# Two sets of fifteen small loads on the load queue of a one-token attention and gated-MLP kernel

## The chip, the cores and the metric

The kernel runs on one core of one Trainium2 chip. The metric is device time in microseconds (us) of one execution, the median of repeated runs. The core has five engines, each with its own list of instructions: TensorE (PE, with PEld for its weight loads), VectorE (DVE), ScalarE (ACT), GpSimd (POOL) and SyncE (SP). They meet through semaphores alone. Loads from the chip's main memory (HBM) run on 16 DMA engines; here nearly all of them are issued by SP, and the page calls their queue q1.

## The reference

One token of width 576 goes through a layer norm, then through an attention over a cache of 8192 keys and values for each of 32 heads, and beside it through a gated MLP; both results are added to the token. Cut to what is computed:

```python
xn = layernorm(x)                                     # 1 x 576
q = (xn @ wq).reshape(32 heads, 128)
p = softmax(q . k_cache * 128**-0.5)                  # 32 heads x 8192 keys
o = p . v_cache                                       # 32 heads x 128
y = x + o.reshape(4096) @ wo + (relu(xn @ W_gate) * (xn @ W_up)) @ W_down
```

All of it is float32. The caches are 268 MB, the four weight matrices the rest of 319 MB, and each byte is used once.

## The kernel before

**Tiles.** The inputs are laid out so that almost every load is one tile of 128 partitions with up to 16384 floats in each (64 KB a partition, 8192 KB a load). Three SBUF tiles, slot0 to slot2, take the loads in turn. First come the query weights and two tiles with gate weights (wq, wqt, wg), then 32 loads from kv: load n brings the keys of head n and the values of the head before it. Then follows vw (values of the last head, the last gate weights and the first nine chunks of output weights, 7968 KB), and then the remaining 59 chunks of output weights from wod. OUT (line 25) cuts these into loads of 28, then 17, 8 and 3, then 2 and 1 chunks; one chunk is 128 x 576 floats, 288 KB.

**The load queue.** `load` (line 165) adds one DMA to SP's list, with a wait and a semaphore. SP works through its list strictly in order. A load waits until its slot is free, which is a mark on PE: ("pm", n - 3) for kv loads, ("pm", H - 2) for the load of 28 chunks, ("pm", H - 1) for those of 17, 8 and 3, and ("first", 8), set when the nine chunks that came with vw are used up, for those of 2 and 1. The last item of SP's list is the store of the result (line 190), which waits for the mark "end".

**A head.** DVE multiplies a tile of keys by the query (`product`, line 296) and sums over the head's width (`sums`, line 301), takes the maximum of each partition (line 302), PE spreads it and DVE reduces it (`bound`, line 305), ACT takes exponentials (`soft`, line 321), and PE multiplies by the values (`values`, line 328, all PE work at line 223). After three heads ACT copies the sums from PSUM to the tile `row` (`rows`, line 325) and PE turns them into columns (`outputs`, mark ("ot", k)). The last such group is k = NIT = 10, with the last two heads: its copy waits for the mark ("V", H - 1) of PE.

**The end.** PE multiplies every chunk of output weights by its column: the first 64 chunks into the bank `acc`, the last four into the bank `fin` (lines 409 to 431). DVE copies `acc` into the tile `both` (line 432, mark "y"), PE adds it to `fin`, DVE copies `fin` to `total4` (line 433, mark "end"), and SP stores it. The tile `both` has no other use, and `row` is not used after ("ot", NIT). A wait in the program is written as a mark; `run` (line 96) turns the marks of one instruction into semaphore waits, one for each semaphore.

Of the kernel before, what the change touches and what calls it, by code (L numbers as in the profile page):

```python
# [9 lines left out]
P = 128  # L10
# [8 lines left out]
NIT = (H - 2) // G  # L19
# [15 lines left out]
STEP = 1  # L35
# [6 lines left out]
class Program:  # L42
# [19 lines left out]
    def add(self, engine, f, waits=(), mark=None, on=None, by=1):  # L62
        to = None
        if mark is not None:
            to = on or engine
            self.sem(to)
            self.counts[to] += by
            assert mark not in self.marks, mark
            self.marks[mark] = (to, self.counts[to])
        self.lists[engine].append((f, tuple(waits), to, by))  # L70
# [41 lines left out]
def build(nc, x, kv, vw, wq, wqt, wg, wod, out):  # L112
    pr = Program(nc)
    add = pr.add

    def sb(name, shape):
        return nc.alloc_sbuf_tensor(name, list(shape), F32).ap()

    def bank(name):
        return nc.alloc_psum_tensor(name, [P, 512], F32).ap()  # L120
# [4 lines left out]
    both = sb("both", [P, N2])  # L125
# [12 lines left out]
    row = sb("row", [P, 576])  # L138
    xr = row[:1, :]
    row = row[:, :512]  # L140
    total4 = sb("total4", [P, Q])
# [12 lines left out]
    bq, bb, bm, bo, bt, acc, fin, bx = [bank(f"bank{i}") for i in range(8)]  # L154
# [3 lines left out]
    ot = bt[:, :G]  # L158
# [6 lines left out]
    def load(name, k, src, waits, on, start=0):  # L165
        dst = slots[k % 3][:, start:start + src.shape[-1]]
        add("sync", lambda e: e.dma_start(dst, src), waits, name, on=on, by=16)  # L167

    def tile(n):
        return slots[(n + 3) % 3]  # L170

    load("wq", 0, wq, (), "dwq")
    load("g0", 1, wqt, (), "dg0")
    load("g1", 2, wg, (), "dg1")
# [4 lines left out]
    for n in range(4, H):  # L179
        load(("t", n), n + 3, kv[n], (("pm", n - 3),), f"land{(n - 1) % G}" if n < H - 1 else "dlast")  # L180
    load(("t", H), H + 3, vw, (("pm", H - 3),), "dvw")
    f = OUT[0][0]
    for k, loads in enumerate(OUT[1:]):
        free = (("pm", H - 2), ("pm", H - 1), ("first", OUT[0][0] - 1))[k]
        i = 0
        for n in loads:
            load(("o", f), H + 4 + k, wod[:, (f - 9) * D:(f - 9 + n) * D], (free,), f"do{f}", i * D)
            i += n
            f += n
    add("sync", lambda e: e.dma_start(out.rearrange("o (j q) -> (o j) q", j=4), total4[0:P:32, :]), ("end",), "out", on="dout", by=16)  # L190


    add("gpsimd", lambda e: e.memset(ident, 0.0), (), "id0")
# [37 lines left out]
    for k in range(36):  # L231
        if k < 32:
            r, a, j = k // 16, k // 4 % 4, k % 4
            mm(("wq", "xz") if k == 0 else (), None, bq[32 * j:32 * j + 32, :], xz[:, a, 5 - r:37 - r],
               slots[0][:, a * 4096 + (4 * r + j) * 512:][:, :512], k < 4, False)
        else:
            j = k - 32
# [3 lines left out]
    def turn(rows, waits, mark):  # L241
        for b in range(4):
            add("tensor", lambda e, b=b: e.transpose(turned[:, b, :], rows[:, b * P:(b + 1) * P], ident),
                waits if b == 0 else (), mark if b == 3 else None)
# [77 lines left out]
                                             bias=nb[h % 2], scale=1.0, accum_out=L[:, i:i + 1]), waits, ("exp", h), on=f"exp{i}", by=STEP)  # L322

    def rows(k, h):
        add("scalar", lambda e: e.copy(row, bo), (("V", h),) + ((("ot", k - 1),) if k else ("pqt",)), ("oc", k), on="oc", by=STEP)  # L325


    def values(i, t, waits, mark, end):
# [22 lines left out]
    for n in range(1, H):  # L351
        k, i = (n - 1) // G, (n - 1) % G
        product(n, keys(n), i, (("t", n),) + ((("q", k + 1),) if i == 0 else ()))
        bound(n - 1)
        if i == 0 and k:
            close(k - 1, G)
        sums(n, keys(n))
        if i == 0 and k < NIT:
            spread(k + 2, [h for h in range(G * k + 4, G * k + 7) if h < H])
        soft(n - 1)  # L360
        if i == G - 1:
            rows(k, n - 1)
    bound(H - 1)
    soft(H - 1)
    rows(NIT, H - 1)
    add("vector", lambda e: e.tensor_copy(gr, bq), ("u3",), "gr")
    pj = turned.rearrange("k b (j r) -> k b r j", j=4)
# [15 lines left out]
    for i in range(G):  # L383
        t = tile(i + 1)
# [20 lines left out]
    f, end = 0, H + FC  # L405
# [3 lines left out]
    for k, loads in enumerate(OUT):  # L409
        t = tile(H)[:, SK + UNITS[3] * 512:] if k == 0 else slots[(H + 3 + k) % 3]  # L410
        i = 0
        for n in loads:
            for m in range(n):
                waits = (("o", f),) if m == 0 and k else ()
# [79 lines left out]
```

## Time and profile before

| what | value |
|---|---|
| median of 3 runs | 745.06 us (744.97 to 745.23) |
| profiled execution, span from first to last instruction | 743.7 us |
| median of the runs less that span | 1.3 us |
| DMA read | 319.16 MB, 429 GB/s over the span |
| busy time of DVE / PE / ACT / POOL | 575.6 / 294.7 / 36.2 / 1.8 us |
| mean granted TensorE clock | 0.674 |

The profile gives the span of its execution and no separate time for it; the runs' median is 1.3 us longer than the span. In the profile a releaser is what ended a wait. SPq and ACTq are the engines' own DMA issues; "us to landing" is counted from an issue until its semaphore is full. A window is a stretch of the span, in us from its start.

### The profile page before, as it was taken

How to read it: one execution, taken by the hardware profiler on the slowest of the kernel's cores; microseconds unless marked ns; L12 is line 12 of the kernel's file. 1: busy time of each engine (PE TensorE's matmuls, PEld its weight loads, DVE VectorE, ACT ScalarE, POOL GpSimd, SP SyncE). 2: the span in 40 equal slices, each digit the busy share in tenths (PEclk: the TensorE clock that was granted, in tenths of full speed). 3: DMA queues.
4: the chain of work that ended last, by engine and by line, in shares of the span. 5: the costliest groups of instructions: out<-in, count | busy, mean ns of one | idle time of the engine just before them, and what ended most of it. 6: DMA issues, size and time to landing. Idle time of an engine off the chain costs nothing.

```text
span 743.7 us, 4003 instructions
## 1 busy us (share of the span) xinstructions
PE 294.7 (40%) x1780; PEld 84.0 (11%) x1780; DVE 575.6 (77%) x169; ACT 36.2 (5%) x113; POOL 1.8 (0%) x9
## 2 busy tenths in 40 slices
PE   1555413253343343343343334324324324334677
PEld 1111100010010010010010001001001001001122
DVE  2000189989999999999999999999999999999610
ACT  2000000010010010010000000001001000000000
POOL 0000000000000000000000000000000000000000
PEclk9977756655565565665666666666566566566689
DMA  9999999999999999999999999999999999999997
GB/s 395 451 420 426 445 444 410 441 451 405 444 448 406 448 441 412 448 437 430 430 441 437 419 441 444 412 441 444 412 444 441 416 448 437 430 430 435 435 424 309
DMA packets 6066, 319.28 MB, mean 429 GB/s; under 512 B 677, under 2 KB 681, under 8 KB 1066
## 3 DMA queue, kind: packets, MB, share of 16 engines
q1 hardware_dynamic: 6056, 319.17, 99.3%
q8 instruction: 6, 0.10, 0.1%
q14 instruction: 2, 0.02, 0.0%
q10 hardware_dynamic: 2, 0.00, 0.0%
HBM read 319.16 MB, written 0.00 MB: 429 GB/s over the span
## 4 chain that ended last, share of the span: by engine, by line
DMA 58%; DVE 37%; PE 4%; issue 0%; ACT 0%; SPq 0%; DVEq 0%
DMA slot<-in_kv 47%; DVE slot L296 19%; DVE s L301 17%; DMA slot<-in_wqt 5%; DMA slot<-in_wod 5%; PE bank L223 4%; DVE mr L302 0%; DVE nb L305 0%; DVE total L310 0%; SPq L167 0%; ACT row L325 0%; DVE both L432 0%; ACT pzs L321 0%; DVE total L314 0%; DVE total L433 0%
## 5 line engine op out<-in xcount | busy, mean ns | idle before, releaser
L296 DVE TENSOR_TENSOR slot<-slot,bank 128x8192 f32<-128x8192 f32 x32 | 278.0, 8686 | 85.8 <-PE bank L223 50.5
L301 DVE TENSOR_REDUCE s<-slot 128x64 f32<-128x8192 f32 x32 | 277.6, 8676 | 0.0
L223 PE MATMUL bank<-slot,pzs 128*12 128x512 f32 x1024 | 181.2, 873 | 205.5 <-ACT pzs L321 205.5
L223 PEld LDWEIGHTS bank<-slot,pzs 128*12 128x12 f32 x1024 | 32.7, 122 | 332.2 <-ACT pzs L321 204.3
L223 PE MATMUL bank<-slot,xz 128*32 128x512 f32 x208 | 37.3, 753 | 31.7 <-DMA slot<-in_wq 12.8
L223 PE MATMUL bank<-ident,mr 128*128 128x128 f32 x64 | 16.3, 339 | 78.2 <-DVE mr L302 78.1
L223 PE MATMUL bank<-l,ones 128*128 128x3 f32 (+1 forms) x22 | 6.2, 354 | 99.9 <-ACT pzs L321 99.9
L321 ACT ACTIVATE pzs<-s,nb 128x64 f32<-128x64 f32 x32 | 11.1, 348 | 470.9 <-DVE nb L305 470.9
L246 DVE TENSOR_SCALAR row<-bank 128x512 f32<-128x512 f32 x1 | 0.7, 692 | 34.4 <-PE bank L223 34.4
L432 DVE COPY both<-bank 128x288 f32<-128x288 f32 x1 | 0.5, 459 | 27.2 <-PE bank L223 27.2
L223 PEld LDWEIGHTS bank<-ident,mr 128*128 128x128 f32 x64 | 9.9, 194 | 100.3 <-DVE mr L302 100.2
L283 ACT ACTIVATE dq<-ident,qs 128x128 f32<-128x128 f32 x32 | 10.7, 392 | 131.6 <-PE bank L223 90.9
L223 PEld LDWEIGHTS bank<-l,ones 128*128 128x128 f32 x22 | 5.3, 299 | 102.8 <-ACT pzs L321 102.0
L223 PEld LDWEIGHTS bank<-slot,xz 128*32 128x32 f32 x208 | 8.5, 133 | 57.7 <-issue 23.7
L223 PE MATMUL bank<-sel,row 128*128 128x3 f32 (+1 forms) x88 | 11.6, 254 | 7.3 <-ACT row L325 7.2
L223 PE MATMUL bank<-slot,os 128*1 128x288 f32 x128 | 10.8, 480 | 5.6 <-DMA slot<-in_wod 5.6
L223 PEld LDWEIGHTS bank<-sel,row 128*128 128x128 f32 x88 | 10.6, 191 | 16.8 <-ACT row L325 16.8
L223 PE MATMUL bank<-slot,hh 128*1 128x288 f32 (+1 forms) x160 | 12.0, 382 | 1.3 <-DMA slot<-in_wod 1.3
L223 PE MATMUL bank<-dq,ones 128*128 128x384 f32 (+1 forms) x24 | 11.4, 560 | 0.0
L223 PE MATMUL bank<-slot,xt 128*32 128x512 f32 x26 | 6.0, 896 | 9.8 <-DMA slot<-in_wqt 9.8
L325 ACT COPY row<-bank 128x512 f32<-128x512 f32 x11 | 6.5, 587 | 70.7 <-PE bank L223 70.7
L305 DVE TENSOR_REDUCE nb<-bank 128x1 f32<-128x128 f32 x32 | 9.1, 284 | 0.9 <-PE bank L223 0.9
(55 smaller groups left out, 52.4 us busy)
## 6 DMA issues: line engine op xcount, KB each, us to landing
slot<-in_wod SPq DMA_DIRECT2D x1, 8064.0 KB, 38.9
slot<-in_vw SPq DMA_DIRECT2D x1, 7968.0 KB, 39.2
slot<-in_wod SPq DMA_DIRECT2D x1, 4896.0 KB, 30.2
slot<-in_wod SPq DMA_DIRECT2D x1, 2304.0 KB, 35.7
slot<-in_wod SPq DMA_DIRECT2D x1, 864.0 KB, 37.2
slot<-in_wod SPq DMA_DIRECT2D x1, 576.0 KB, 25.7
slot<-in_kv SPq DMA_DIRECT2D x32, 39.7
slot<-in_wod SPq DMA_DIRECT2D x1, 288.0 KB, 26.0
```

Of the source, the lines that this page charges most:

```text
L223: add("tensor", lambda e: e.matmul(o, lhsT, rhs, start=start, stop=stop), waits, mark)
L246: add("vector", lambda e: e.tensor_scalar_mul(row, bq, SCALE), ("pq", "n7"), "qr")
L283: add("scalar", lambda e, m=m, h=h: e.activation(dq[:, m, :], ident, AF.Copy, scale=qs[:, h:h + 1]), (free,) if m == 0 else (), ("dq", k) ...
L296: add("vector", lambda e: e.tensor_mul(k3, k3, qb[:, m, None, :].to_broadcast([P, C, DH])), waits, ("mul", h))
L301: add("vector", lambda e: e.reduce_sum(s, k3, axis=AX.X), (("mul", h),), ("sum", h))
L305: add("vector", lambda e: e.tensor_reduce(nb[h % 2], pm, axis=AX.X, op=ALU.max, negate=True), (("pm", h),), ("nb", h))
L321: add("scalar", lambda e: e.activation(pz[:, i, :, 4 * G - 4:4 * G], s2[h % 2].rearrange("p (c b) -> p c b", b=4), AF.Exp, bias=nb[h % 2], ...
L325: add("scalar", lambda e: e.copy(row, bo), (("V", h),) + ((("ot", k - 1),) if k else ("pqt",)), ("oc", k), on="oc", by=STEP)
L432: add("vector", lambda e: e.tensor_copy(both, acc[:, :N2]), ("sums",), "y")
```

## The change

A helper `few` adds fifteen DMAs to SP's list, which load 15 rows, then 14, and so on down to 1 row, each into its own columns of a tile, and each with a semaphore of its own. It is called twice. Set a goes behind the load of vw: each row has 16 floats (64 bytes), the destination is `both`, there is no wait, and the last copy of `rows` (k = NIT) gets the fifteen marks of the set as waits. Set b goes behind the load of the last chunk: each row has 32 floats (128 bytes), the destination is `row`, each of its DMAs waits for ("ot", NIT), and the store of the result gets the fifteen marks of the set as waits. The source is always the start of wod; what the small loads bring is not read.

```diff
+    def few(name, t, n, waits=()):
+        for k in range(15, 0, -1):
+            add("sync", lambda e, k=k: e.dma_start(t[:k, (k - 1) * n:k * n], wod[:k, :n]), waits, ("few", name, k), on=f"few{name}{k}", by=16)
+
...
     load(("t", H), H + 3, vw, (("pm", H - 3),), "dvw")
+    few("a", both, 16)
     f = OUT[0][0]
...
-    add("sync", lambda e: e.dma_start(out.rearrange("o (j q) -> (o j) q", j=4), total4[0:P:32, :]), ("end",), "out", on="dout", by=16)
+    few("b", row, 32, (("ot", NIT),))
+    add("sync", lambda e: e.dma_start(out.rearrange("o (j q) -> (o j) q", j=4), total4[0:P:32, :]),
+        tuple(("few", "b", k) for k in range(15, 0, -1)) + ("end",), "out", on="dout", by=16)
...
     def rows(k, h):
-        add("scalar", lambda e: e.copy(row, bo), (("V", h),) + ((("ot", k - 1),) if k else ("pqt",)), ("oc", k), on="oc", by=STEP)
+        add("scalar", lambda e: e.copy(row, bo), (("V", h),) + ((("ot", k - 1),) if k else ("pqt",)) + (tuple(("few", "a", m) for m in range(1, 16)) if k == NIT else ()), ("oc", k), on="oc", by=STEP)
```

On SP, from the load of vw to the end, the list before was this (the last column pair is rows x floats in a row, and the square bracket names the semaphores waited for):

```order
L167 DMA slot<-in_vw 128x15936 [waits s_tensor]
L167 DMA slot<-in_wod 128x16128 [waits s_tensor]
L167 DMA slot<-in_wod 128x9792 [waits s_tensor]
L167 DMA slot<-in_wod 128x4608 [waits s_tensor]
L167 DMA slot<-in_wod 128x1728 [waits s_tensor]
L167 DMA slot<-in_wod 128x1152 [waits s_tensor]
L167 DMA slot<-in_wod 128x576 [waits s_tensor]
L190 DMA out_y<-total 4x144 [waits s_vector]
```

With the change the small loads of set b stand between the last load and the store; this is the end of SP's list now, from the load with 5 rows on:

```order
L174 DMA row<-in_wod 5x32 [waits s_tensor]
L174 DMA row<-in_wod 4x32 [waits s_tensor]
L174 DMA row<-in_wod 3x32 [waits s_tensor]
L174 DMA row<-in_wod 2x32 [waits s_tensor]
L174 DMA row<-in_wod 1x32 [waits s_tensor]
L196 DMA out_y<-total 4x144 [waits s_fewb7,s_fewb6,s_fewb8,s_fewb5,s_fewb9,s_fewb4,s_fewb10,s_fewb3,s_fewb11,s_fewb2,s_fewb12,s_fewb1,s_fewb13,s_vector,s_fewb14,s_fewb15]
```

The store's waits stand in the order in which SP meets them: the mark "end" (s_vector) comes fourteenth, and two of set b come after it. On ACT nothing is added but waits; these are its last five rows now, of which the last is the copy of `rows` for the last two heads:

```order
L290 ACTIVATE dq<-ident,qs 128x128 [waits s_tensor]
L328 ACTIVATE pzs,l<-s,nb 128x16x4 [waits s_tensor,s_vector] x3
L332 COPY row<-bank 128x512 [waits s_tensor]
L328 ACTIVATE pzs,l<-s,nb 128x16x4 [waits s_tensor,s_vector] x2
L332 COPY row<-bank 128x512 [waits s_fewa8,s_fewa9,s_fewa7,s_fewa10,s_fewa6,s_fewa11,s_fewa5,s_fewa12,s_fewa4,s_fewa13,s_fewa3,s_fewa14,s_fewa2,s_fewa15,s_fewa1,s_tensor]
```

The fifteen waits on set a come ahead of the wait for PE, which before was the copy's only one. PE, DVE and POOL have the instructions that they had, in the same order.

## The prediction

> **What bounds the kernel now.** First the page's head, its DMA row and its queues; then the chain of work that ended last.
>
> ```profile
> span 743.7 us, 4003 instructions
> DMA  9999999999999999999999999999999999999997
> DMA packets 6066, 319.28 MB, mean 429 GB/s; under 512 B 677, under 2 KB 681, under 8 KB 1066
> q1 hardware_dynamic: 6056, 319.17, 99.3%
> ...
> q10 hardware_dynamic: 2, 0.00, 0.0%
> 293.76 39.65 DMA slot<-in_kv
> ...
> 351.82 39.65 DMA slot<-in_kv
> ...
> 701.42 35.70 DMA slot<-in_wod
> 737.12 0.04 issue
> 737.16 2.66 PE bank L223 x40
> 739.83 0.02 issue
> 739.85 0.47 DVE both L432
> 740.32 0.04 issue
> 740.37 1.32 PE bank L223 x32
> 741.69 0.02 issue
> 741.71 0.31 DVE total L433
> ```
>
> SP's queue, q1, keeps the 16 DMA engines busy for 99.3% of the span, and no slice but the last is below 9 tenths. In the middle a wait ends at 293.76 + 39.65 = 333.41 and the next such one at 391.47, three loads later: 58.06 / 3 = 19.35 us for 8192 KB. So time on this queue is time of the kernel, up to the last load. The end is read from the timeline:
>
> ```profile
> 661.37 0.33 SPq L167 DMA_DIRECT2D slot<-in_vw  x1
> 680.71 34.88 SPq L167 DMA_DIRECT2D slot<-in_wod  x6
> 701.64 0.19 ACT L321 ACTIVATION_READ_ACCUMULATOR pzs<-s,nb 128x1 f32 x1
> 710.53 0.59 ACT L325 COPY row<-bank 128x512 f32<-128x512 f32 x1 [8.71 <-PE bank L223]
> 711.17 1.05 PE L223 MATMUL bank<-sel,row 128*128 128x2 f32 x8
> 719.65 6.83 PE L223 MATMUL bank<-slot,os 128*1 128x288 f32 x74 [4.90 <-DMA slot<-in_wod]
> 741.21 0.10 PEld L223 LDWEIGHTS bank<-slot,hh 128*1 128x1 f32 x8 [0.25 <-DMA slot<-in_wod]
> 741.71 0.31 DVE L433 COPY total<-bank 128x144 f32<-128x144 f32 x1 [1.40 <-PE bank L223]
> 742.04 0.62 SPq L190 DMA_DIRECT2D out_y<-total  x1
> ```
>
> The load of 28 chunks lands at 719.65, the last chunk at 741.21; PE waits for both. After the last chunk come 0.5 us of matmuls, DVE's copy until 742.02, and the store. The store's landing ends the span. A DMA delayed by some time before 741.21 delays the end by the same time; work behind the last chunk has 742.02 - 741.21 = 0.81 us of cover.
>
> **The change, part by part.** Nothing is removed. Each set adds 15 issues on SP and 15 + 14 + ... + 1 = 120 rows on q1, and how many marks these bring is shown by the two small DMAs of before: the one-row load of x is all of q10, with 2 packets, so one row and one mark. The store's packets are seen in two narrow windows:
>
> ```profile
> DMA packets 7, 0.00 MB, mean 29 GB/s; under 512 B 3, under 2 KB 7, under 8 KB 7
> q1 hardware_dynamic: 7, 0.00, 12.3%
> ...
> q1 hardware_dynamic: 1, 0.00, 2.8%
> ```
>
> The first (743.26 to 743.34) has four rows of 576 bytes and three marks: 12.3% of 16 x 0.08 us is 157 ns. The second (743.35 to 743.37) has the fourth mark alone: 2.8% of 16 x 0.02 us is 9 ns. So a row here costs (157 - 3 x 9) / 4 = 33 ns, a mark 9 ns, and a DMA has as many marks as rows when these are under 16. The small rows of 64 and 128 bytes are not in this trace: I bound one between the mark (9 ns) and the 576-byte row (33 ns), and take 12 ns, near the mark, since 64 and 128 bytes are nearer to 4 than to 576.
>
> *SP's issues.* A DMA right behind another took 0.43 us, the four-row store 0.62:
>
> ```profile
> 701.42 0.43 SPq L167 DMA_DIRECT2D slot<-in_wod  x1
> 714.79 0.81 SPq L167 DMA_DIRECT2D slot<-in_wod  x2
> ```
>
> Fifteen with 0.05 us between them take 15 x 0.48 = 7.2 to 15 x 0.67 = 10.1 us. Set a is issued from 661.7 to at most 671.8; what is queued behind it on SP is the load of 28 chunks, released at 680.71, so 8.9 us are left. Even if that load went out late, the queue has work until vw has landed, at 661.37 + 39.2 = 700.6 (the page's row for vw, below). Set b is issued behind the last load: 714.79 + 0.81 = 715.6, so until at most 725.7; its mark ("ot", NIT) is set at 711.17 + 1.05 = 712.22, earlier. Behind it stands only the store, released at 742.02. Price of both: nothing; without this cover an issue of over 1.7 us each (26.4 us / 15) would show.
>
> ```profile
> slot<-in_vw SPq DMA_DIRECT2D x1, 7968.0 KB, 39.2
> SPq L190 <- DVE total L433: 26.4, 1, 26.4
> ```
>
> *Set a on the DMA engines.* Its packets lie between vw and the next load on a queue that never idles, so they are paid in full on the engine that carries them. The worst placed engine gets one row of each of the 15 loads, an even spread gives 120 / 16 = 7.5. The price is 7.5 x (9 + 9) = 0.14 us at least where the slowest engine has an average share, 15 x (33 + 9) = 0.63 us at most, and zero if the engine that lands last is one that gets no rows. With 12 ns and all fifteen rows it is 15 x 21 = 0.31 us; I take **0.3 us**, and keep 0 and 0.63. The Trainium skill (DMA: Bandwidth & Descriptors, "Why a DMA increments its semaphore by 16 and not by 1") says that a queue like SP's takes the lowest-numbered engines, as many as the largest number up to 16 that divides the rows; the trace agrees on the number (four marks for four rows), and no row of it shows which engines. By that rule one engine has all fifteen rows and the sum is 0.31; by an even spread it would be 0.16.
>
> *The copy on ACT.* The waits on set a come first. Set a lands a fraction of a microsecond after vw, near 701; ACT is idle from 701.83 to 710.53 waiting for PE. The waits are over in that gap: nothing. Were they late by up to 8.7 us, nothing would move; behind the copy PE has another 4.9 us of idle before 719.65.
>
> *Set b.* It queues behind the last chunk. On the engine with all fifteen rows its last mark follows 0.31 us after that chunk, 0.63 at most, so it lands near 741.5 and at the latest at 741.84. The store's own mark "end" comes at 742.02: hidden, with 0.2 to 0.5 us to spare. Behind that mark two waits on set b remain, both satisfied: between 0 and 0.05 us, the step between two DMAs on SP; I take 0.
>
> Sum: 743.7 + 0.3 = 744.0 for the span, and with the 1.3 us around it, which the runs show, 745.06 + 0.3 = **745.4 us**. By the bounds 745.1 to 745.7, and the runs before spread over 0.26 us.
>
> **The rivals.** *First: each extra load costs a step of its own on the queue, beyond its packets.* The five loads from 719.65 to 741.21 move 31 chunks, 9.14 MB, in 21.56 us. At the pace of the kv loads (19.35 us for 8.39 MB, with one step in each) they would take 21.09; with four steps more than the kv loads' share the excess of 0.47 us makes at most 0.12 us a step. Fifteen steps are then 1.8 us for set a, and set b ends 1.8 us after 741.21, or 1.0 past the mark "end": 2.8 in all, **747.9**, slower. It crosses 0.2% (1.5 us, about what a measurement of this kernel can tell from no change) at 0.077 us a step. For it speaks the excess; against it that engines land unevenly, which gives an excess without any step. Chance 0.10.
>
> *Second: the marks are served one at a time.* If an engine held what is behind a mark until the rows ahead are confirmed, each small load would cost the time from the store's last packet, 743.36, to its landing at the span's end, 743.7: about 0.35 us. Fifteen make 5.2 us for set a, and 5.2 - 0.8 = 4.4 for set b: **754.7**. The Trainium skill (Perfetto Trace Analysis, "DMA Instruction — HWDGE (DVE, Sync)") says that the last descriptor of a DMA writes the semaphore only after the write before it is confirmed, and that this can be a surprisingly long delay. By that rule, if it holds up the queue, the time is this rival's; the trace speaks against the holding up, since a step costs 0.12 us at most there. Chance 0.05.
>
> *Third: the queue takes few loads at a time.* Six loads are out together in the trace (the six on wod, 701 to 716, with no long issue). Set a makes it 17 with the two big ones. If eight were the limit, SP would stall on set a until vw lands at 700.6, then issue its last eight in some 4 us and only then the load of 28 chunks, whose packets start about 1 us later: 5 us of idle queue. Set b would stall likewise and have seven issues left after 741.2: 3.5 us and a landing of about 1.2 more, 3.9 past "end". Sum 9, **754**. Chance 0.05.
>
> *Fourth: less than the packets.* The last engine carries none of the rows: 745.1. That lies within the forecast.
>
> **How the numbers follow.** Forecast, with the fourth case, 0.79: 744.9 to 746.5. First rival 0.10, second and third 0.10 together. Faster for a reason not seen, such as engines that end in another order, 0.01. The forecast alone leaves out 0.21, so the range takes in the first rival: 744.9 to 748.0. The first and the other rivals lie over the bound; a little of the forecast goes over either edge: faster 0.02, within 0.2% 0.80, slower 0.18.
>
> **What would show it.** The page has 6066 + 480 = 6546 packets, 677 + 480 = 1157 of them under 512 B. The load of 28 chunks is still issued at 680.7 and lands 0 to 0.6 us later than 719.65; ACT's last copy still waits for PE; the store's releaser is still DVE at line 433. A landing of vw's successor over 1.5 us late speaks for the first or second rival, an issue of a small load that lasts microseconds for the third, and a store released by a DMA says that set b outlived its cover. What would make the prediction wrong is any cost of a small load over 0.08 us on one engine.

## The result and the profile after

The changed kernel takes **748.34 us** (748.25 to 748.44, 4 runs) against 745.07 (744.97 to 745.23, 4 runs): 3.3 us slower, ratio 1.0043 with a 95% interval of 1.0032 to 1.0055. The forecast was 745.4, the range ended at 748.0. The profiled execution of the change took 748.25, with a span of 746.7, so 1.5 us lie outside the span where 1.3 lay before; the span itself grew by 3.0. The intervals below leave out one execution of set a alone, which took 1333.5 us.

The page's head, its DMA packets and its queues:

```profile
span 746.7 us, 4049 instructions
DMA packets 6547, 319.31 MB, mean 428 GB/s; under 512 B 1157, under 2 KB 1161, under 8 KB 1546
q1 hardware_dynamic: 6536, 319.19, 99.1%
...
q14 instruction: 3, 0.02, 0.0%
```

The 480 packets that were forecast are there, all under 512 bytes; one packet more is an instruction fetch on q14, which had two before. The timeline of the end, with the lines that answer to those of before:

```profile
661.59 0.33 SPq L167 DMA_DIRECT2D slot<-in_vw  x1
661.96 5.39 SPq L174 DMA_DIRECT2D both<-in_wod  x15
...
680.99 33.19 SPq L167 DMA_DIRECT2D slot<-in_wod  x6
...
709.11 0.59 ACT L332 COPY row<-bank 128x512 f32<-128x512 f32 x1 [7.54 <-PE bank L230]
...
714.22 11.91 SPq L174 DMA_DIRECT2D row<-in_wod  x15
...
720.77 7.31 PE L230 MATMUL bank<-slot,os 128*1 128x288 f32 x74 [7.45 <-DMA slot<-in_wod]
...
742.09 0.10 PEld L230 LDWEIGHTS bank<-slot,hh 128*1 128x1 f32 x8 [0.27 <-DMA slot<-in_wod]
742.59 0.31 DVE L440 COPY total<-bank 128x144 f32<-128x144 f32 x1 [1.41 <-PE bank L230]
745.00 0.62 SPq L196 DMA_DIRECT2D out_y<-total  x1
```

The load of 28 chunks is issued 0.28 us later than before (680.99 for 680.71), while vw still had 20 us to run, and PE has it 1.12 us later (720.77 for 719.65). The last chunk is 0.88 us late (742.09 for 741.21), and so is DVE's copy (742.90 for 742.02). Then SP, which went 0.02 us after that copy before, goes 2.10 us after it. From the store's issue to the end it is 1.7 us in both. So of the 3.0 us in the span 0.88 are set a's and 2.08 are the store's wait for set b. What SP waited for, and what the DMA engines did meanwhile, by the waits of SP and by windows (the last two numbers of a window are the DMA engines' busy share and GB/s):

```profile
SPq L106 <- DMA row<-in_wod: 17.9, 2, 17.7
...
739.00:741.70 2.70, 2.36 (x52) 0.93 (x44) 0.46 (x1) 0.00 (x0) 0.00 (x0) 1.00 0.56 205
741.70:745.00 3.30, 0.82 (x24) 0.21 (x13) 0.31 (x1) 0.00 (x0) 0.00 (x0) 1.00 0.00 0
```

All packets of set b have been started by 741.70, none is left, and yet SP is released only near 745: in these 3.3 us no data is left to move, and what SP still waits for are marks. The trace's records of semaphores show them. The last increments of the small loads' semaphores, from the load with 15 rows to that with one, and the length of the first packet of the load of 28 chunks on each of the 16 engines, in us:

```text
set a, last increment   700.82 700.99 701.16 701.33 701.51 701.68 701.84 702.04
                        702.25 702.44 702.13 702.30 701.96 702.14 702.18
set b, last increment   742.26 742.47 742.67 742.87 743.07 743.27 743.47 743.66
                        743.87 744.07 743.91 744.10 744.12 744.29 744.47
first packet behind set a, after    4.23 4.08 3.86 3.77 3.68 3.64 3.48 3.36
                                    2.81 2.65 2.48 2.41 2.40 2.40 2.39 2.39
first packet of that load, before   2.38 to 2.39 on all sixteen
```

Where two marks in a row are of one engine, they come in steps of 0.16 to 0.21 us, not of 9 ns (the list shows the last mark of each load, and jumps where that is another engine's). The first big packet behind set a is held by up to 1.85 us, in grades: from 4.23 to 2.48 in ten steps of 0.175 on the average. The starts of the packets ahead show which engine is which: fifteen small rows run ahead of the packet of 4.23, ten ahead of that of 3.64, five ahead of that of 2.48. The load's last landing, 720.73, is that of the engine with ten rows: the engine with fifteen was held longer, but had been about 1.2 us ahead of the last.

### The profile page after: what moved, and what is told of

The parts are those of the page before. It is cut to its first block, busy times and chain, and to the rows that moved or that the text cites. A ratio compares the mean times of both kernels' runs of the same rounds, so it can differ in the third digit from the quotient of the medians.

```text
span 746.7 us, 4049 instructions
## 1 busy us (share of the span) xinstructions
PE 298.9 (40%) x1780; PEld 84.1 (11%) x1780; DVE 575.5 (77%) x169; ACT 36.2 (5%) x113; POOL 1.8 (0%) x9
## 4 chain that ended last, share of the span: by engine, by line
DMA 57%; DVE 38%; PE 3%; issue 0%; SPq 0%; DVEq 0%
DMA slot<-in_kv 47%; DVE slot L303 19%; DVE s L308 18%; DMA slot<-in_wqt 5%; DMA slot<-in_wod 5%; PE bank L230 3%; DVE mr L309 0%; DVE nb L312 0%; SPq L167 0%; DVE total L317 0%; DVE both L439 0%; DVE total L321 0%; DVE total L440 0%; DVE os L322 0%; DVEq L106 0%
## 5 line engine op out<-in xcount | busy, mean ns | idle before, releaser
L230 PE MATMUL bank<-slot,pzs 128*12 128x512 f32 x1024 | 187.5, 900 | 204.1 <-ACT pzs L328 204.1
L230 PE MATMUL bank<-sel,row 128*128 128x3 f32 (+1 forms) x88 | 11.6, 254 | 7.3 <-ACT row L332 7.2
```

The lines of the kernel that those rows point to most:

```text
L230: add("tensor", lambda e: e.matmul(o, lhsT, rhs, start=start, stop=stop), waits, mark)
```

## The experiments

Theory M: on one engine the marks of small loads are served one after another, about 0.18 us each; some are absorbed, what lies behind more of them is held. What counts is the number of marks on the busiest engine, and how early that engine is through with the big loads. Rivals: R, the small rows are slow and the mark costs nothing; T, all marks go through one place, so their total counts; and, by sums, that each load costs the same wherever it stands. All runs are compared with the kernel before on the same chip (745.0 in each group); intervals are of the ratio. Edits are shown against the change, cut to the lines that matter.

**Each set alone.** `a_only` drops set b, `b_only` drops set a, each with its waits.

> Set a alone, no set b. All theories hold that the marks or rows of set a delay the load stream. Theory M (on each engine the mark of a small load holds what is behind it for about 0.18 us until its row is confirmed; reading ahead hides some of it): the load of 28 chunks lands about 1.1 us later than before and the end moves by 0.7 to 1.1 us, to 745.8 to 746.2. If set a costs only its packets (15 x 13 ns): +0.2, 745.3.

> Set b alone, no set a. Theory M: 15 marks of 0.18 us on the engine with all fifteen rows, so the last mark 2.5 to 2.8 us behind the last chunk at 741.2, near 743.9; then SP walks through its waits in up to 0.5 us: store at 744.0 to 744.5 instead of 742.04, so +2.0 to +2.5, 747.1 to 747.6. If sets a and b are independent, the gain of this run and that of set a alone add up to 3.3.

Set a alone: 746.12, ratio 1.0015 (1.0005 to 1.0025), as expected. Set b alone: 746.42, 1.0018 (1.0009 to 1.0028), which is 0.7 below what was expected. Together 2.5 by the medians, not 3.3: the sets do not look independent, though the intervals would allow it; the run on stacking below tests this. The trace of `b_only` says why its part was too high: the engine with all fifteen rows is one of those that end the last chunk early. Its last mark came at 742.30; the last mark of the set came at 742.99, on an engine that is late but has ten.

**Marks or rows.** `b_one_mark` loads 15 separate rows on each of 16 partitions with one DMA, so 240 rows, 15 of them and one mark on each engine; `a_one_mark` does the same in set a's place, with rows of 64 bytes.

```diff
-    few("b", row, 32, (("ot", NIT),))
+    add("sync", lambda e: e.dma_start(row[:16, :510].rearrange("p (c w) -> p c w", w=34)[:, :, :32],
+                                      wod[:16, :960].rearrange("p (c w) -> p c w", w=64)[:, :, :32]), (("ot", NIT),), ("few", "b"), on="fewb", by=16)
```

> Set b as one load: 16 partitions with 15 separate rows of 128 bytes each, so each engine has 15 rows but one mark. Theory M: one mark, so it lands about 0.4 us behind the last chunk, before the mark end: no change, 745.0 to 745.2. Theory R (a row under 512 bytes takes about 0.18 us to write, the mark nothing): 15 rows on every engine, the same 2.7 us behind the last chunk, store at about 744.0, 747.0.

> Set a alone as one load: 16 partitions with 15 separate rows of 64 bytes each, so every engine has 15 rows and one mark. Theory M (the marks): no packet behind it is held by over 0.2 us, 745.0 to 745.3 (15 rows of 13 ns add 0.2). Theory R (the rows): every engine is held as the busiest one of set a was, by 1.85 us, and the end moves by as much or more than with set a alone: 746.1 to 747.

745.37, 1.0004 (0.9994 to 1.0013), and 745.35, 1.0004 (0.9995 to 1.0013): twice the rows without the marks cost about 0.35 us, not told apart from nothing. R falls, for both sets: its 747.0 and 746.1 lie outside the intervals. The first packet behind `a_one_mark` is held by 0.15 to 0.33 us on the sixteen engines.

**The busiest engine or the total.** `b_one_row` makes every load of set b one row, so 15 rows and 15 marks in all.

```diff
-            add("sync", lambda e, k=k: e.dma_start(t[:k, (k - 1) * n:k * n], wod[:k, :n]), waits, ("few", name, k), on=f"few{name}{k}", by=16)
+            add("sync", lambda e, k=k: e.dma_start(t[:1, (k - 1) * n:k * n], wod[:1, :n]), waits, ("few", name, k), on=f"few{name}{k}", by=16)
```

> Set b as 15 loads of one row each: 15 rows and 15 marks in all, all on one engine. Theory M: what counts is the marks on the busiest engine, still 15; the last mark 2.5 to 2.8 us behind that engine's share of the last chunk, so +1.2 to +2.5 by where this engine stands among the sixteen: 746.3 to 747.6. Theory T (marks of all engines go through one place, 120 in 2.6 us, 22 ns each): 15 marks take 0.3 us and are hidden, 745.1.

745.66, 1.0009 (0.9999 to 1.0018): less than the band of M, more than T's. The time alone does not decide; the trace does. Its timeline, and the fifteen last increments of its loads:

```profile
740.88 0.11 PEld L229 LDWEIGHTS bank<-slot,hh 128*1 128x1 f32 x8 [0.24 <-DMA slot<-in_wod]
741.38 0.31 DVE L439 COPY total<-bank 128x144 f32<-128x144 f32 x1 [1.38 <-PE bank L229]
742.66 0.61 SPq L195 DMA_DIRECT2D out_y<-total  x1
```

```text
740.01 740.19 740.37 740.55 740.74 740.91 741.08 741.27 741.45 741.63 741.81 741.99 742.17 742.34 742.52
```

With nothing on the other engines the step is still 0.18 us, where T has 22 ns. The store goes 0.14 us after the last of them, 0.97 after DVE's copy. The engine that has the rows was through with the last chunk near 739.8, a microsecond before the latest (740.84), which hid that much of its 2.7 us. My band had allowed for too little of this lead.

**Stacking.** `a_one_row_b` has set b as in the change, and set a with one row in each load: `few` takes `m = k if name == "b" else 1` rows.

> Both sets, but set a as 15 loads of one row each, so that it puts its 15 marks on one engine and nothing on the others; set b as in the change. Theory M with stacking (both sets fall on the same engine, which set a makes late by 1.9 us and set b by 2.6 us more): last chunk lands about 0.6 us late, last mark of set b near 744.3, store at 744.3 to 744.9, so +2.5 to +2.9: 747.5 to 747.9. Additive theory (each set costs what it costs alone, set b 1.4 us, and set a with an eighth of its rows at most 0.6): 747.0 or less.

748.06, 1.0039 (1.0025 to 1.0053): nearly the whole loss comes back with an eighth of set a's rows. All five runs (747.78 to 748.40) lie above the additive theory's 747.0, which the interval just reaches; the trace decides. Behind set a one single first packet is held, with 4.22 us; the other fifteen take 2.38 to 2.39. At the end the latest landing of the last chunk is 742.08, and the fifteen marks of set b on one engine run from 742.27, one step behind it, to 744.78. So both sets fall on the same engine: set a uses up the lead that it had, and set b's fifteen marks follow on that. This agrees with the Trainium skill (DMA: Bandwidth & Descriptors, "Why a DMA increments its semaphore by 16 and not by 1"), by which a queue like SP's takes the lowest-numbered engines. The trace names no engine and shows only that it is the same one.

**How many are free.** `a_five` has five loads in set a (5 to 1 rows) and no set b; `b_eight` has eight in set b and no set a.

```diff
-        for k in range(15, 0, -1):
+        for k in range(5, 0, -1):
```

> Set a alone with five loads of 5 to 1 rows, so at most five marks on an engine. In the trace of the change the first packet behind set a was held by 1.85 us on the engine with the most marks and by about 0.18 less with each mark less, down to nothing at about four or five marks. Theory M with this allowance: no packet held by over 0.2 us, no change: 744.9 to 745.2. If each mark costs its share of the 1.1 us of set a alone: 745.35.

> Set b alone with eight loads of 8 to 1 rows. In the trace of set b alone the engines with few rows end the last chunk late, near 741.0, the one with all rows early, near 739.8. With eight loads the busiest engine is through at 739.8 + 8 x 0.18 = 741.3, the late ones with two marks or fewer at 741.5, all before the mark end: 745.0 to 745.3. If the cost goes with the number of loads: 8/15 of 1.4, 745.8.

745.10, 1.0000 (0.9991 to 1.0010), and 745.16, 1.0002 (0.9993 to 1.0011). Both as M has it. The medians lie below a cost in proportion (745.35 and 745.8), but the intervals reach that far; the traces speak against it. Behind five marks the first packet was held by 0.14 us at most, and the last chunk was not late (landed 741.10, before 741.17). In `b_eight` the last mark came at 741.48, under the cover of DVE's copy, which SP waited for:

```profile
741.65 0.31 DVE L439 COPY total<-bank 128x144 f32<-128x144 f32 x1 [1.41 <-PE bank L229]
742.05 0.61 SPq L195 DMA_DIRECT2D out_y<-total  x1
```

**Another queue.** `b_act` issues set b from ACT, behind its last copy, without set a: `add("scalar", ...)` in `few`, called behind `rows(NIT, H - 1)`.

> Set b alone, issued by ACT behind its last copy instead of by SP, so in another queue on the same engines, beside the big loads rather than behind the last of them. Theory M: each mark is served while a big packet moves, no mark is left after the last chunk, the store comes right after the mark end: 744.9 to 745.3. If the marks wait for the engine's other queue to run dry, or hold its packets as in set a: 746.0 or more.

745.29, 1.0004 (0.9995 to 1.0013): as expected at the upper end. The small loads now run beside the big ones; the last mark came at 738.26, and the store 0.10 us after DVE's copy.

**The wait's own part.** `ab_one_sem` and `ab_one_sem_2` are the same kernel, both sets with one semaphore for all of set b; `after_again` is the change once more.

```diff
-        tuple(("few", "b", k) for k in range(15, 0, -1)) + ("end",), "out", on="dout", by=16)
+        (("few", "b", 1), "end"), "out", on="dout", by=16)
```

> Both sets as in the change, but the fifteen loads of set b share one semaphore, and the store waits for its full count, so it has two waits instead of sixteen. If SP's walk through the waits costs the 0.5 us between the last mark (744.47) and the store (745.00): store at 744.5, 747.8. If the walk costs nothing and the last mark really comes at 744.9: 748.3, as the change.

> The change again, beside the other three. 748.1 to 748.5. In the first trace SP stood still for 0.47 us between two waits whose semaphores were long full, and an extra instruction block was fetched then (745.69). If that is a border in SP's code, the same gap stands at the same wait again; if it was an accident, it is gone.

> Both sets, one semaphore for set b, a second time. If the gap is a border in SP's code, seven instructions less move it behind the store and do not remove it: the store is 0.5 to 0.7 us earlier than in the change, but the time outside the span grows by about 0.2, so 747.7 to 748.2. If only the last mark of set b counts: no difference from the change in the trace either.

748.31 (747.70 to 748.34), 748.27 (748.10 to 748.49) and 748.08 (747.93 to 748.37). In the traces of the change SP's waits on set b are recorded at these times, when they are over, two semaphores in one wait (rows of their loads; "end" is the mark):

```text
after        7: 743.89  6,8: 744.09  5,9: 744.16  4,10: 744.23  3,11: 744.30  2,12: 744.77  1,13: 744.86  end,14: 744.94  store: 745.00
after_again  7: 743.85  6,8: 744.06  5,9: 744.13  4,10: 744.20  3,11: 744.33  2,12: 744.80  1,13: 744.90  end,14: 744.97  store: 745.04
```

Where the marks are there, steps are 0.06 to 0.09 us, but before the wait for 2 and 12 rows SP stands for 0.47, though both its semaphores were full by 744.29 in `after` and by 744.49 in `after_again`. The trace of `a_one_row_b`, with the same list on SP, has it at the same wait. So it is no accident of one execution. With one semaphore the store goes 2.27 and 2.55 us after the last chunk's landing instead of 2.96 and 3.02; but the time outside the span is 1.71 instead of 1.55, and the medians differ from the change by 0.0 and 0.2, inside the spread. The list of waits costs 0.4 to 0.75 us of the trace and is not shown to be worth anything in the time.

`ab_store_free` lets the store wait for "end" alone and puts the waits on set b behind it.

> Both sets as in the change, but the store waits for the mark end alone; the waits on set b stand behind the store. Theory M: store at 742.9 (set a's 0.9 us alone), but its marks come behind those of set b on the same engines, so the span ends at 744.6 to 745.0 instead of 746.7: 746.2 to 746.6. If the last chunk's landing were the main cost of the change: over 747.5.

747.64, 1.0035 (1.0022 to 1.0048): 0.7 better than the change, a microsecond worse than expected. The store went at 743.33 and its last mark came at 745.09, 1.76 us later (1.65 before), so the marks ahead of it hardly held it. But the edit also put the signal that ends the program behind the waits, which were over at 745.30, with the same 0.47 us of standstill one wait earlier (before 3 and 11), and the span ended at 746.0. In the trace the store's last mark is 1.6 us earlier than in the change (745.09 for 746.67); the time shows 0.7 of that, and what it would show without the moved signal is open.

**Is the row's write in the 0.18 us?** `b_wide` gives set b rows of 2304 bytes in a free part of slot2, `b_wide_spread` puts the same rows on every eighth partition (`t[0:8 * k:8, ...]`).

```diff
-    few("b", row, 32, (("ot", NIT),))
+    few("b", slots[2][:, 2048:], 576, (("ot", NIT), ("first", 8)))
```

> Set b alone with rows of 2304 bytes instead of 128 (into a part of slot2 that is free by then; the loads wait for the mark first too). A row of this size took 93 ns in the last chunk. If the mark's 0.18 us begin when its row has been written, the step on an engine is 0.27 us, the fifteen take 4.1 us: store near 743.9 or later, +1.9 to +2.4, 746.9 to 747.4. If rows go on while a mark waits, the step stays 0.18 us: as set b alone, 746.4.

> Set b alone with rows of 2304 bytes on partitions 0, 8, 16 and so on instead of 0, 1, 2. If the crowding in the run with wide rows came from the neighbouring partitions, the last chunk lands near 741.2 again. Step on the engine with all rows: 0.18 us if rows go on while a mark waits (746.3 to 746.6), 0.27 if a mark's time begins when its row is written (747 or more). If the crowding stays, the cause is the rows' source or their size, and the time is near 749 again.

748.95, 1.0050 (1.0033 to 1.0067), and 747.57, 1.0035 (1.0022 to 1.0048): neither hits its band for 0.18. `b_wide` is beyond both bands, and `b_wide_spread` lies in that for 0.27, but for another reason. The timeline of the two, in this order:

```profile
743.62 0.10 PEld L229 LDWEIGHTS bank<-slot,hh 128*1 128x1 f32 x8 [1.04 <-DMA slot<-in_wod]
...
746.25 0.61 SPq L195 DMA_DIRECT2D out_y<-total  x1
```

```profile
742.02 0.10 PEld L229 LDWEIGHTS bank<-slot,hh 128*1 128x1 f32 x8 [0.76 <-DMA slot<-in_wod]
...
744.43 0.58 SPq L195 DMA_DIRECT2D out_y<-total  x1
```

Here the last chunk itself is late, by 2.4 and 0.8 us. The big packets took longer (one of 4608 bytes up to 0.71 us in `b_wide`, 0.18 before) while engines that were ahead already had their wide rows; on every eighth partition two thirds of the delay are gone. So the wide rows crowd the packets of the engines that are behind, by their partitions for the most part; where they meet, no run shows. The step of the marks on the engine with all rows stayed 0.18 us in both once the crowd was over (in `b_wide_spread` 742.06, 742.24, 742.42, 742.60, 742.79, 742.97), as with 64 and 128 bytes. So the mark's time does not grow with its row.

## Why the prediction was wrong

**What bounds the kernel: right.** The queue's time was the kernel's time; what delayed a DMA before the last chunk moved the end by as much.

**SP's issues: right in price, wrong in detail.** The forecast was 7.2 to 10.1 us for a set. Set a took 5.4, set b 11.9, since the last three issues stalled:

```profile
718.74 1.59 SPq L174 DMA_DIRECT2D row<-in_wod  x1
718.74 4.48 SPq L174 DMA_DIRECT2D row<-in_wod  x2
720.38 5.75 SPq L174 DMA_DIRECT2D row<-in_wod  x2
```

They took 1.59, 2.85 and 2.86 us: with six big loads and twelve small ones out the queue took no more at once. It was not a load that had to land first, since none landed between 720.73 and 729. The last two issues took the time of two packets of the load of 17 chunks (1.45 us each in the trace), and each small load brings two packets, a row and a mark. So there is a limit, but it looks like one of packets on an engine and not the third rival's limit of loads; no run varies it. SP's cover hid it.

**ACT's copy: right.** It waited for PE, as before (709.11, idle 7.54 us); its waits on set a were over at 702.8.

**Set a on the DMA engines: the path right, the mark's size wrong.** The step that failed is "a row here costs 33 ns, a mark 9 ns". Rows were even cheaper than that (in the records a row and its mark's packet take 13 ns together), and `a_one_mark` cost 0.33 us, not told apart from nothing. The mark was not: 9 ns is how long its packet is recorded, 0.18 us is how far apart the marks of small loads come on one engine. That is also over the 0.08 us which the prediction named as what would make it wrong. The four marks of the store arrived within 0.06 us (743.63 to 743.69), closer than the 0.16 us or more between marks of one engine, and the big loads' marks on one engine stand at least 0.7 us apart (8 rows of 93 ns), so the trace of before had no two marks close together on one engine, and I took a duration for a rate. The price of set a was 0.3, at most 0.63; it is 0.9 in the trace of the change and 1.1 in the time of set a alone. It is less than 15 x 0.18 = 2.7 since about five marks are absorbed (`a_five`; held 1.85 us at the most) and since the busiest engine was about a microsecond ahead of the last: the landing that PE waited for was that of the engine with ten marks.

**Set b: the same term, and a cover that set a had spent.** The step "hidden, with 0.2 to 0.5 us to spare" rested on fifteen marks in 0.31 us. They take 2.5, and the last came 1.57 us behind DVE's copy. Alone set b cost 1.4; behind set a its engine starts late, so both sets together cost 0.8 more than the sum of the two. The sign that the prediction had named for this came: SP's wait for the store was ended by a DMA. The prediction looked at each set against the end of the slowest engine, and at neither against the engine on which both fall.

**Two waits behind "end": the step about right, the order wrong.** They were to cost up to 0.05, and from the wait with "end" to the store it was 0.06. But SP was to stand at "end" when set b was long in. In fact it was still in the waits ahead of "end" when the last mark came, and the store followed that mark by 0.53 us, 0.30 of it the rest of the standstill from 744.30 to 744.77. Runs with one semaphore do not show that this costs time outside the trace.

**The rivals.** The first rival had a price of 0.12 us a step, taken from the excess of 0.47 us over the five last loads, and its 747.9 came within 0.5 of the result. That was luck: its mechanism, a step on the whole queue, was not what happened, since engines with few marks were hardly held. The range had been drawn to take in this rival, so that it ended so near the result is luck too. The second rival had the mechanism, marks served one at a time, with 0.35 us, twice the size, and without the absorbed five. It was given 0.05 because the five last loads show almost no step; with their marks on one engine 0.7 to 11.6 us apart, they could not. The Trainium skill (DMA: Bandwidth & Descriptors, "Anatomy of one DMA — SWDGE (gpsimd) path") calls the bubble of a semaphore write tiny, about one cycle; the section is on loads of the gpsimd path, and these are SP's. The trace of before agrees for marks far apart: behind vw's mark the first packet took 2.38 to 2.39 us, as later ones did (2.38). For marks of small loads in a row it was 0.18 us, and the measurement decides.

What the 0.18 us are is left open: that they do not grow with the row speaks against the row's own write as their main part, but no run takes the mark away from its row, or has two small loads on one engine without a mark between them. So a cost of going from one load to the next on an engine is not told apart from a cost of the mark.

## What to carry to other kernels

Count completion marks on each DMA engine, not bytes or rows, and set them against when that engine is through with its other work: here five in a row were free, and each further one held whatever lay behind by about 0.18 us, while the busiest engine's lead hid a microsecond of it. The loads with fewer than 16 rows here all fell on the same engines, so the two sets added up there, 40 us apart; one load with many rows, or small loads issued early on another queue beside big packets, cost at most some 0.35 us, not told apart from nothing. When a trace gives a duration for one thing, ask whether it ever shows two of them in a row before using it as a rate.

## What was not expected of the hardware

- A mark every 0.18 us on one DMA engine, for rows of 64, 128 and 2304 bytes alike.
- A limit of the load queue: with six big loads and twelve small ones out, an issue of 0.3 us took up to 2.9, the time of two packets ahead of it.
- SP's standstill of 0.47 us at the same wait in all three traces with the change's list on SP, and one wait earlier where the store stood ahead of the waits. An extra instruction fetch appears in each of these traces (745.43 to 745.69), but 0.6 to 0.9 us after the standstill. A border in SP's code is possible; no run moved it alone, so this is argued and not shown.
- With rows of 2304 bytes on fifteen neighbouring partitions, the big loads' packets of 4608 bytes took up to 0.71 us for 0.18; on every eighth partition the last chunk's delay fell from 2.4 to 0.8 us.
